# Attention into a mixture of experts: PSUM as four shared tiles of two banks, one eviction over both banks, and a new order

## The chip, the cores and the metric

One core of one Trainium2 chip runs the whole program. The metric is the device time of one execution in microseconds (us). The engines are TensorE (PE: matmuls, with its weight loads as PEld), VectorE (DVE), ScalarE (ACT), GpSimd (POOL) and SyncE (SP), which issues the transfers. Matmul results land in PSUM, which has 8 banks of 512 fp32 values on each of 128 partitions; DVE and ACT copy them on to SBUF. "Quadrants" below are the four 64x64 parts of TensorE's 128x128 array: the half of the partitions that a matmul reads, by the half of the PSUM partitions that it writes.

## The reference

```python
# attention: batch 8, 8 heads, 576 rows, 64 columns a head, fp32
q_d, k_d, v_d = (mean over 4 neighbouring rows of q, k, v)      # 144 pooled rows
out_up    = repeat(softmax(scale * q_d k_d^T) v_d, 4 rows)
out_local = softmax(scale * q k^T where |i - j| < 4) v
x = out_up + out_local                                          # (8, 576, 512)
# mixture of 4 experts of 64 columns, the 2 best of each row by x @ w_gate
q, k, v = x @ wq[e], x @ wk[e], x @ wv[e]
ye = causal_softmax(scale * q k^T) @ v @ wo[e]
out = sum over the two chosen e of w_e * ye
```

## The kernel before

**Stages.** Each of the 8 batches goes through three stages, which run staggered, so that three batches are in work at a time. Stage 1 works on one pair of heads at a time (4 pairs). `s1_local` (L688) makes the banded scores, 20 matmuls of 64 columns. `s1_down` (L725) pools q and k and makes the pooled scores: three query tiles t = 0, 1, 2, each for two heads h, of 144 columns (L773). `s1_out` (L807) transposes both probability tiles ("tp", five blocks of 128x128 each) and multiplies them by v ("o1", "o1d"), which gives x and its split into a high and a low part. Stage 2 projects x to q, k ("pj", L879) and v with the gate ("pv", `s2_v`, L910). Stage 3 is the causal attention: `s2_scores` (L1013), unit u = 1 to 4 of two or three query tiles, `s2_trans` (L1065; "tq", five jobs for each batch and pair of experts), `s2_av` (L1118) and the output projection `s2_out` ("po", L1153; in the last batch `s2_out_cut`, L1171).

**Order.** Every step is an `op` with the engine or engines that may run it, a planned cost, what it reads and writes, and the PSUM and SBUF buffers that it takes. `Plan.schedule` (L245) plays the ops through by these planned costs and writes the instructions in that order, once, when the program is built: of the ops that are ready and whose buffers are free, an engine takes the one of the lowest number in `ORDER`. On TensorE it may prefer another one. An op of the same `MODE` as the last goes ahead if its number is no more than `SWM` above the best (L347), and a change of mode is charged by `SWX` (L376). `MODE` knows "dense" (the projections, on the whole array) and "quarter" (everything on quadrants); the transposes "tp" and "trans", which read one half of the partitions and write all 128, count as "quarter". Where the plan sees too little matmul work, it puts in a filler, a matmul of zeros ("wu", L662).

**PSUM.** There are two pools: `big`, two tiles of two banks (local scores, x, projections, the longest score tile), and `small`, four tiles of one bank (L499 to L503). Pooled scores, transposes and `s2_av` take two small tiles each, one for each half; `s2_v` takes one.

**Evictions.** `transpose` (L553) writes the two halves of a block to two tiles. So each transposed job has two copies to SBUF, `tp_ev` (L816, L826) and `t_ev` (L1115), which the plan gives to ACT or DVE one by one; the copies stand in the profile under the helper's lines, L509 on ACT and L511 on DVE. The pooled scores' maxima are two reductions (L777), one for each small tile.

**The quadrants of the pooled scores.** At L773 head h reads half h of the partitions and writes half h, for each of the three tiles. The local scores swap the heads in half of their tiles (L700), the causal scores in every other tile (L1024).

Of the kernel before, what the change touches and what calls it, by code (L numbers as in the profile page):

```python
# [7 lines left out]
F32 = mybir.dt.float32  # L8
# [451 lines left out]
def dve(n):  # L460
    return 65 + n / 0.96
# [11 lines left out]
def tile_attn_then_moe(ctx: ExitStack, tc: tile.TileContext, qT, kT, v, wqk, wvg, wo, out):  # L473
# [25 lines left out]
    def big(name):  # L499
        return buf(psB, [128, 1024], name, 2, tag="big", fifo=False)  # L500
# [800 lines left out]
```

## Time and profile before

| | |
|---|---|
| time, median of 3 runs | 503.04 us (499.98 to 506.42) |
| the profiled execution's own time | 501.08 us |
| its span, first to last instruction | 499.3 us |
| mean granted TensorE clock | 0.997 of full speed |
| busy share of the span | PE 98%, PEld 85%, DVE 79%, ACT 67%, POOL 63% |

A busy TensorE isn't a TensorE at its peak: a matmul counts as busy for its whole latency, and the next one can start long before it ends. What the engine delivers is read from the distances between starts.

### The profile page before, as it was taken

How to read it: one execution, taken by the hardware profiler on the slowest of the kernel's cores; microseconds unless marked ns; L12 is line 12 of the kernel's file. 1: busy time of each engine (PE TensorE's matmuls, PEld its weight loads, DVE VectorE, ACT ScalarE, POOL GpSimd, SP SyncE). 2: the span in 40 equal slices, each digit the busy share in tenths (PEclk: the TensorE clock that was granted, in tenths of full speed). 3: DMA queues.
4: the chain of work that ended last, by engine and by line, in shares of the span. 5: the costliest groups of instructions: out<-in, count | busy, mean ns of one | idle time of the engine just before them, and what ended most of it. 6: DMA issues, size and time to landing. Idle time of an engine off the chain costs nothing.

```text
span 499.3 us, 20630 instructions
## 1 busy us (share of the span) xinstructions
PE 487.9 (98%) x8391; PEld 423.7 (85%) x8393; DVE 392.2 (79%) x1256; ACT 334.8 (67%) x1150; POOL 314.7 (63%) x451
## 2 busy tenths in 40 slices
PE   8889999999999999999999999999999999999988
PEld 4678997998988988998898888997988888988776
DVE  8899689976867998679887689859995978547770
ACT  2987588767757678556766587656894567455763
POOL 6789968965855689566785468644773664124231
PEclk9989999999999999999999999999999999999999
DMA  8875445431523333242444053414331100100112
GB/s 218 266 210 176 116 131 163 118 99 44 174 90 123 107 114 113 78 152 61 129 123 136 29 152 102 151 55 150 94 123 61 55 1 3 74 26 13 49 51 95
DMA packets 43463, 52.72 MB, mean 106 GB/s; under 512 B 3304, under 2 KB 26344, under 8 KB 43368
## 3 DMA queue, kind: packets, MB, share of 16 engines
q1 hardware_dynamic: 43368, 51.40, 34.6%
q8 instruction: 66, 1.08, 0.9%
q14 instruction: 29, 0.24, 0.1%
HBM read 40.90 MB, written 9.44 MB: 101 GB/s over the span
## 4 chain that ended last, share of the span: by engine, by line
PE 83%; DVE 10%; ACT 3%; DMA 2%; issue 1%; POOL 1%; SPq 0%; DVEq 0%; ACTq 0%; POOLq 0%
PE pj L879 21%; PE po L1160 9%; PE pv L920 9%; PE sq L1024 8%; PE o L1137 6%; PE tq L556 6%; PE tp L556 5%; PE o L838 4%; PE scd L773 4%; PE sc L700 3%; PE o L844 2%; PE pv L929 1%; DVE pr L1042 1%; PE po L1184 1%; DMA wst<-in_wo_dram 1%
## 5 line engine op out<-in xcount | busy, mean ns | idle before, releaser
L1045 ACT ACTIVATE pr<-pr,pst 128x192 f32<-128x192 f32 (+8 forms) x144 | 80.0, 558 | 26.6 <-DVE pst L1042 24.6
L1053 POOL TENSOR_SCALAR pr<-pr,pst,gt 128x192 f32<-128x192 f32 (+8 forms) x88 | 58.7, 671 | 56.7 <-DVE pst L1050 39.6
L879 PE MATMUL pj<-xh,wqk_h 128*128 128x320 f32 (+1 forms) x248 | 77.8, 314 | 0.0
L1042 DVE CUSTOM_DVE_ANT_0 pr<-sq,causal_t 128x192 f32<-128x192 f32 (+8 forms) x144 | 65.8, 483 | 11.2 <-PE sq L1024 10.6
L879 PE MATMUL pj<-xl,wqk_h 128*128 128x320 f32 (+1 forms) x248 | 73.2, 295 | 0.0
L879 PE MATMUL pj<-xh,wqk_l 128*128 128x320 f32 (+1 forms) x248 | 73.1, 295 | 0.0
L1024 PE MATMUL sq<-k,q 64*64 64x256 f32 (+6 forms) x768 | 57.3, 374 | 0.2 <-DVE x L856 0.2
L879 PEld LDWEIGHTS pj<-xh,wqk_h 128*128 128x128 f32 x248 | 46.6, 188 | 4.2 <-issue 1.0
L862 POOL TENSOR_TENSOR xl<-x,xh 128x576 fp32r<-128x576 f32 x29 | 41.3, 1426 | 9.2 <-ACT xh L861 9.2
L879 PEld LDWEIGHTS pj<-xh,wqk_l 128*128 128x128 f32 x248 | 46.7, 188 | 0.0
L879 PEld LDWEIGHTS pj<-xl,wqk_h 128*128 128x128 f32 x248 | 46.6, 188 | 0.0
L785 ACT ACTIVATE dp<-scd,dst 128x144 f32<-128x144 f32 x96 | 35.2, 374 | 10.8 <-DVE dst L780 10.3
L721 POOL TENSOR_TENSOR lp<-lp,lst 128x640 f32<-128x640 f32 x27 | 34.6, 1283 | 10.9 <-DVE lst L720 8.4
L1024 PEld LDWEIGHTS sq<-k,q 64*64 64x64 f32 x768 | 32.2, 133 | 10.8 <-issue 1.0
L556 PE MATMUL tq<-ident,pr 64*128 64x64 f32 x736 | 38.5, 232 | 2.1 <-ACT oh L1148 0.7
L511 DVE COPY ptb<-tq 128x192 f32<-128x192 f32 (+4 forms) x95 | 29.7, 348 | 12.6 <-PE tq L556 12.2
L556 PEld LDWEIGHTS tq<-ident,pr 64*128 64x128 f32 x736 | 29.1, 138 | 11.6 <-issue 3.5
L920 PE MATMUL pv<-wvg_h,xh 128*128 128x260 f32 x128 | 37.5, 293 | 0.0
L1149 POOL TENSOR_TENSOR ol<-oc,oh 128x256 fp32r<-128x256 f32 (+1 forms) x30 | 23.9, 799 | 20.9 <-ACT oh L1148 18.3
L752 POOL TENSOR_TENSOR lr<-lr 128x512 f32<-128x512 f32 x28 | 36.3, 1296 | 0.0
L920 PE MATMUL pv<-wvg_h,xl 128*128 128x260 f32 x128 | 36.2, 283 | 0.0
L920 PE MATMUL pv<-wvg_l,xh 128*128 128x260 f32 x128 | 36.2, 283 | 0.0
(178 smaller groups left out, 1514.5 us busy)
## 6 DMA issues: line engine op xcount, KB each, us to landing
lv<-in_v_dram SPq DMA_DIRECT2D x64, 160.0 KB
lq<-in_qT_dram SPq DMA_DIRECT2D x32, 292.0 KB
lk<-in_kT_dram SPq DMA_DIRECT2D x32, 292.0 KB
out_dram<-ot SPq DMA_DIRECT2D x28, 288.0 KB
lr<-in_v_dram SPq DMA_DIRECT2D x28, 256.0 KB
lr<-in_v_dram SPq DMA_DIRECT2D x28, 64.0 KB
wst<-in_wqk_dram SPq DMA_DIRECT2D x1, 1024.0 KB
vx<-vg SPq DMA_DIRECT2D x8, 128.0 KB
```

Of the source, the lines that this page charges most:

```text
L556: T.transpose(pss[x]()[:, z:z + 64], data[r, 0:128], ident[r, r])
L721: op("l_nrm", "GV", (pool_tt(n), dve(n)), lambda e: eng[e].tensor_tensor(p(), p(), st[:, :, 2:3].to_broadcast([128, NT, W]), op=OP.mult), ...
L752: eng[e].tensor_tensor(vr[:, :, 0:2, :], vr[:, :, 0:2, :], vr[:, :, 2:4, :], op=OP.add)
L785: A.activation(p()[:, t, :], scs[t // 2]()[:, SD * (t % 2):SD * (t % 2) + SD], AF.Exp, bias=st[:, t, 4:5], scale=1.0 / 128.0, accum_out=st ...
L862: op("xl", "GV", (1360, dve(576)), lambda e: eng[e].tensor_tensor(xl(), x(), xh()[:, 0:S].bitcast(F32), op=OP.subtract), r=[x, (xh, 0)], w ...
L879: T.matmul(ps()[:, H0 + n0:H0 + n1], ww[:, c, w0 + 128 * p:w0 + 128 * p + 128], xx[b, c]()[:, n0:n1], start=(i == 0), stop=(i == 3 * NP - 1))
L920: T.matmul(ps()[:, :260], xx[b, c]()[:, 128 * t:128 * t + 128], ww[:, c, :], start=(i == 0), stop=(i == 3 * NP - 1))
L1024: T.matmul(pss[x]()[halves[e ^ (x % 2)], at + to:at + to + n1 - n0], q()[r, 64 * t:64 * t + 64], k()[r, n0:n1], start=True, stop=True)
L1042: op("s_max", "V", dve(n) + 4, lambda x=x, t=t, n=n, src=src: V.tensor_tensor_reduce(rows_of[t], src(), causal_t[:, S - 64:S + 256] if t = ...
L1045: op("s_exp", "A", 281 + n / 1.2, lambda x=x, t=t, n=n: A.activation(rows_of[t], rows_of[t], AF.Exp, bias=st[:, x, 4:5], scale=-1.0, accum ...
L1053: op("s_nrm", "GV", (327 + n / 1.2 + max(0, n - 384) * 1.1, 189 + n / 1.92), lambda g, x=x, t=t, n=n: eng[g].tensor_scalar(rows_of[t], row ...
L1160: T.matmul(ps()[:, H1 + n0:H1 + n1], ww[:, p, 128 * c:128 * c + 128], xx[b, p]()[:, n0:n1], start=(i == 0), stop=(i == 5))
```

## The change

- PSUM is one pool of four tiles of two banks. What took two small tiles takes one tile and uses both banks; `s2_v` puts two of its five row blocks into one tile, one in each bank; scores of units 1 to 3 put their tiles in the two banks of one tile, unit 4 takes two tiles.
- `tp_ev` and `t_ev` are one copy over both banks instead of two. `v_ev` is one copy for two row blocks, and the transfer `v_cp`, which read block 0 and 2 after the third, is issued after the fourth. The pooled maxima are one reduction instead of two.
- In the last pooled query tile the heads are swapped: head h writes half 1 - h. The rows of that tile stand swapped from then on, and the blocks of "pd" are put in another order (`PD0` to `PD4`, `of_head`), so that the products are the same.
- The plan: transposes are a third mode, "column", with its own charges for a change of mode and an `SWM` of 15.6; some planned costs and the fillers' constants differ; `ORDER` is new throughout (2725 numbers before, 2533 after). `SHIFT`, `LU` and the other tables are the same.

```diff
-FR, TGT, TGT0, T0, TGT2, DW = -7.7, 3150.0, 3400.0, 450400.0, 3700.0, 16.5
+FR, TGT, TGT0, T0, TGT2, DW = -1.1, 3150.0, 3400.0, 152400.0, 3700.0, 10.9
...
-MODE = {"local": "quarter", "down": "quarter", "o1": "quarter", "o1d": "quarter", "av": "quarter", "scores": "quarter", "tp": "quarter", "trans": "quarter",
+MODE = {"local": "quarter", "down": "quarter", "o1": "quarter", "o1d": "quarter", "av": "quarter", "scores": "quarter", "tp": "column", "trans": "column",
...
+       (None, "column"): 95.0, ("dense", "column"): 90.0, ("column", None): 100.0, ("column", "dense"): 92.0,
+       ("column", "quarter"): 95.0, ("quarter", None): 165.0, ("quarter", "dense"): 180.0, ("quarter", "column"): 105.0}
+LAG = {"scores": 85.0, "down": 60.0, "local": 50.0, "o1d": 20.0, "tp": 85.0, "trans": 85.0}
-SWM = {None: 5.1, "quarter": 1.6, "column": 4.1, "dense": 4.9}
+SWM = {None: 0.8, "quarter": 1.2, "column": 15.6, "dense": 5.1}
...
-    psB = ctx.enter_context(tc.tile_pool(name="psB", bufs=2, space=bass.MemoryType.PSUM))
-    psT = ctx.enter_context(tc.tile_pool(name="psT", bufs=4, space=bass.MemoryType.PSUM))
+    psB = ctx.enter_context(tc.tile_pool(name="psB", bufs=4, space=bass.MemoryType.PSUM))
...
-    def transpose(pss, z, data):
+    def transpose(ps, z, data):
         for x, r in enumerate(halves):
-            T.transpose(pss[x]()[:, z:z + 64], data[r, 0:128], ident[r, r])
+            T.transpose(ps()[:, 512 * x + z[x]:512 * x + z[x] + 64], data[r, 0:128], ident[r, r])
...
-        op("c_ge", "V", 560, above, r=cks, w=ges, alloc=ges)
-        op("c_pool", "V", 930, fill_pool, r=cks + ges, w=[(PL, 1)])
+        op("c_ge", "V", 1150, above, r=cks, w=ges, alloc=ges)
+        op("c_pool", "V", 2020, fill_pool, r=cks + ges, w=[(PL, 1)])
...
-        scs = [small("scd") for _ in range(2)]
+        scs, at = big("scd"), 512 - SD
...
-                    T.matmul(scs[t // 2]()[r, SD * (t % 2):SD * (t % 2) + SD],
+                    T.matmul(scs()[halves[h ^ (t // 2)], at * t:at * t + SD],
                              qd()[r, min(NQD * t, SD - 64):min(NQD * t, SD - 64) + 64], kd()[r, 0:SD] if t else kd()[r, WT:WT + SD], start=True, stop=True)
-        op("down", "T", 370, mm, r=[qd, kd], w=scs, alloc=scs + [p])
-        for x, n in ((0, 2), (1, 1)):
-            op("d_max", "V", dve(n * SD), lambda x=x, n=n: V.tensor_reduce(
...
+        op("down", "T", 440, mm, r=[qd, kd], w=[scs], alloc=[scs, p])
+        op("d_max", "V", dve(3 * SD), lambda: V.tensor_reduce(
+            scs()[:, 1000:1003], strided(scs()[:, 0:SD], (at, 3)), op=OP.max, axis=AX.X, negate=True), r=[scs], w=[(scs, "m")])
...
-        op("tp", "T", 20 * QT, tr, r=[p], w=pss, alloc=pss + [pt])
-        for x in range(2):
-            op("tp_ev", "AV", (act(5 * TQ), dve(5 * TQ)), lambda e, x=x, pss=pss: copy(
-                e, pt()[:, x], pss[x]()[:, 0:320].rearrange("p (j q) -> p j q", q=64)[:, :, 0:TQ]), r=[pss[x]], w=[(pt, x)])
+        op("tp", "T", 10 * QT + 50, tr, r=[p], w=[ps], alloc=[ps, pt])
+        op("tp_ev", "AV", (act(10 * TQ), dve(10 * TQ)), lambda e, ps=ps: copy(
+            e, pt(), strided(ps()[:, 0:TQ], (512, 2), (64, 5))), r=[ps], w=[pt])
...
-        pss = [(big if t == NU - 1 else small)("sq") for t in ts[:2]]
-        pss += [pss[0]] * (len(ts) - 2)
+        own = [big("sq") for _ in range(2 if u == 4 else 1)]
+        pss = [(own[0], 0), (own[1], 0) if u == 4 else (own[0], 1), (own[0], 0)][:len(ts)]
...
-            for h in range(2):
-                op("t_ev", "AV", (act(k) + m, dve(k) + m), lambda e, h=h, ev=ev: ev(e, h), r=[pss[h]],
-                   w=[(PT[b, p, x[0]], (x[0], x[2], x[3], h ^ x[6])) for x in runs])
+            op("t_ev", "AV", (act(k) + m, dve(k) + m), lambda e, ev=ev: ev(e), r=[ps],
+               w=[(PT[b, p, x[0]], (x[0], x[2], x[3], x[6])) for x in runs])
```

(before the last lines stands `k, m = 128 * len(js), ...` in place of `k, m = 64 * len(js), ...`)

## Rows read from the trace of the kernel before

**Rows 1.** The page's first two parts: busy time of each engine; then, in 40 slices of the span, TensorE's busy share in tenths and its granted clock in tenths of full speed.

```profile
PE 487.9 (98%) x8391; PEld 423.7 (85%) x8393; DVE 392.2 (79%) x1256; ACT 334.8 (67%) x1150; POOL 314.7 (63%) x451
...
PE   8889999999999999999999999999999999999988
...
PEclk9989999999999999999999999999999999999999
```

**Rows 2.** The page's fourth part, the chain that ended last: shares of the span by engine and by line.

```profile
PE 83%; DVE 10%; ACT 3%; DMA 2%; issue 1%; POOL 1%; SPq 0%; DVEq 0%; ACTq 0%; POOLq 0%
PE pj L879 21%; PE po L1160 9%; PE pv L920 9%; PE sq L1024 8%; PE o L1137 6%; PE tq L556 6%; PE tp L556 5%; PE o L838 4%; PE scd L773 4%; PE sc L700 3%; PE o L844 2%; PE pv L929 1%; DVE pr L1042 1%; PE po L1184 1%; DMA wst<-in_wo_dram 1%
```

**Rows 3.** Groups by line, TensorE alone: line, operation, out<-in, shape and count | busy us, mean ns of one | idle time before them and what ended it.

```profile
L556 PE MATMUL tq<-ident,pr 64*128 64x64 f32 x736 | 38.5, 232 | 2.1 <-ACT oh L1148 0.7 <-DVE oc L1146 0.5 <-DVE ptb L511 0.4
...
L773 PE MATMUL scd<-kd,qd 64*64 64x144 f32 x384 | 31.1, 290 | 0.0
...
L556 PE MATMUL tp<-ident,dp 64*128 64x64 f32 x320 | 17.5, 232 | 1.2 <-DVE vd L511 0.8 <-ACT dp L794 0.2 <-DVE pt L511 0.2
L556 PE MATMUL tp<-ident,lp 64*128 64x64 f32 x320 | 16.8, 231 | 0.3 <-DVE pst L1042 0.3
...
L662 PE MATMUL wu<-zero 128*128 128x512 bf16 x36 | 10.0, 398 | 0.1
```

**Rows 4.** The timeline of TensorE, three stretches: start us, length of the merged piece us, line, out<-in, shape, count of instructions. A matmul of fp32 stands as two instructions, its two passes.

```profile
12.99 0.91 PE L773 MATMUL scd<-kd,qd 64*64 64x144 f32 x12
13.83 1.83 PE L758 MATMUL pv<-lv,pool 128*128 128x128 f32 x14
...
202.21 0.26 PE L838 MATMUL o<-pt,lv 64*64 64x58 f32 x1
202.21 0.28 PE L773 MATMUL scd<-kd,qd 64*64 64x144 f32 x1
...
202.33 0.29 PE L773 MATMUL scd<-kd,qd 64*64 64x144 f32 x2
...
203.38 0.47 PE L844 MATMUL o<-pd,vd 64*64 64x144 f32 x8
```

**Rows 5.** The timeline of TensorE again: one job of transposes between quadrant work, two jobs between projections, and the first transposes of the span.

```profile
15.88 0.27 PE L556 MATMUL tp<-ident,dp 64*128 64x64 f32 x1 [0.22 <-ACT dp L794]
...
53.82 0.41 PE L838 MATMUL o<-pt,lv 64*64 64x58 f32 x16
54.16 0.52 PE L556 MATMUL tp<-ident,dp 64*128 64x64 f32 x10
54.61 0.48 PE L844 MATMUL o<-pd,vd 64*64 64x144 f32 x8
...
205.23 0.28 PE L879 MATMUL pj<-xh,wqk_l 128*128 128x256 f32 x1
205.34 0.28 PE L879 MATMUL pj<-xl,wqk_h 128*128 128x256 f32 x1
205.56 0.53 PE L556 MATMUL tp<-ident,dp 64*128 64x64 f32 x10
205.92 0.48 PE L556 MATMUL tp<-ident,lp 64*128 64x64 f32 x10
206.32 0.42 PE L879 MATMUL pj<-xh,wqk_h 128*128 128x320 f32 x1
206.58 0.31 PE L879 MATMUL pj<-xh,wqk_l 128*128 128x320 f32 x1
206.73 0.31 PE L879 MATMUL pj<-xl,wqk_h 128*128 128x320 f32 x1
```

**Rows 6.** Groups by line and form, DVE and ACT: copies out of PSUM and the two reductions of the pooled scores (busy us, mean ns of one | idle before).

```profile
L511 DVE COPY pt<-tp 128x290 f32<-128x290 f32 x35 | 15.1, 451 | 4.9 <-PE tp L556 4.8
L777 DVE TENSOR_REDUCE scd<-scd 128x2 f32<-128x288 f32 x32 | 14.8, 461 | 7.9 <-PE scd L773 5.6 <-ACT dp L785 1.1 <-ACT lp L711 1.0
...
L509 ACT COPY pt<-tp 128x290 f32<-128x290 f32 x29 | 11.1, 404 | 6.1 <-PE tp L556 6.0
...
L509 ACT COPY ot<-po 128x576 f32<-128x576 f32 x17 | 10.8, 638 | 6.3 <-PE po L1160 5.6 <-ACT pr L1045 0.7
...
L777 DVE TENSOR_REDUCE scd<-scd 128x1 f32<-128x144 f32 x32 | 9.8, 306 | 0.2
...
L511 DVE COPY ot<-po 128x576 f32<-128x576 f32 x11 | 8.3, 754 | 1.8 <-PE po L1160 1.2 <-ACT pr L1045 0.3
```

**Rows 7.** The timeline of all engines near the end of the span, where the last batch's transposes stand alone.

```profile
483.19 0.87 PE L556 MATMUL tq<-ident,pr 64*128 64x64 f32 x18 [0.44 <-DVE ptb L511]
483.81 0.82 DVE L511 COPY ptb<-tq 128x320 f32<-128x320 f32 x2 [0.31 <-PE tq L556]
483.85 0.70 ACT L509 COPY ptb<-tq 128x320 f32<-128x320 f32 x2 [0.43 <-PE tq L556]
484.32 0.43 PE L556 MATMUL tq<-ident,pr 64*128 64x64 f32 x6 [0.27 <-ACT ptb L509]
```

**Rows 8.** Busy time of each engine by stretch (PE, PEld, DVE, ACT, POOL, with counts; then the granted clock, the DMA share and GB/s).

```profile
0.00:15.00 15.00, 12.65 (x185) 8.04 (x186) 13.28 (x43) 4.58 (x14) 10.37 (x39) 1.00 0.90 240
...
25.00:30.00 5.00, 3.75 (x72) 3.24 (x70) 3.94 (x10) 4.23 (x15) 3.68 (x4) 0.66 0.84 222
...
480.00:490.00 10.00, 8.15 (x172) 6.51 (x164) 4.79 (x16) 5.54 (x19) 3.65 (x5) 1.00 0.07 24
```

More of the change, by code (lines that the diff above doesn't have):

```diff
@@ L353, in schedule @@
                         best = dense
-                    if e == "T" and free["tr"] + free["big"] > 0 and fill(t, best):
-                        best = self.filler(free["tr"] > 0)
+                    if e == "T" and free["big"] > 0 and fill(t, best):
+                        best = self.filler()
                         left[best.allocs[0]] = 1
@@ L497, in buf, with strided, bank @@
         return b
+    def strided(a, *dims):
+        return bass.AP(tensor=a.tensor, offset=a.offset, ap=[list(a.ap[0])] + [list(d) for d in dims] + [list(a.ap[1])])
     def big(name):
[L500 to L503 removed]
+        return buf(psB, [128, 1024], name, 4, tag="big", fifo=False)
+    def bank(ps, x):
+        return lambda: ps()[:, 512 * x:512 * x + 512]
     eng = {"V": V, "G": G}
@@ L535, in tile_attn_then_moe @@
     V.memset(zero, 0.0)
-    wu = psT.tile([128, 512], F32, name="wu", tag="tr", bufs=4)
+    wu = psB.tile([128, 1024], F32, name="wu", tag="big", bufs=4)
     for _ in range(NW0):
-        T.matmul(wu, zero[:, :128], zero, start=True, stop=True)
+        T.matmul(wu[:, 0:512], zero[:, :128], zero, start=True, stop=True)
     ci = wk.tile([128, 128], I32, name="ci", tag="up")
@@ L656, in needs, with filler @@
         return [(WTS, (id(whi), c)) for c in range(whi.shape[1])]
-    def filler(one):
-        o, ps = Op(), small("wu") if one else big("wub")
+    def filler():
+        o, ps = Op(), big("wu")
         o.kind, o.eng, o.cost, o.prio, o.seq = "warm", "T", 216, 0.0, 0
@@ L801, in s1_down, with of_head, tr @@
         LD[b, c] = (p, vd)
-    def strided(a, *dims):
-        return bass.AP(tensor=a.tensor, offset=a.offset, ap=[list(a.ap[0])] + [list(d) for d in dims] + [list(a.ap[1])])
+    PD0, PD1, PD2, PD3, PD4 = (0, 4), (4, 1), (3, 3), (1, 0), (2, 2)
+    def of_head(a, h, z0, z1, n):
+        a0 = a[:, 5 * h + z0[h], :]
+        return bass.AP(tensor=a0.tensor, offset=a0.offset,
+                       ap=[list(a0.ap[0]), [(z1[h] - z0[h]) * NQD, n], list(a0.ap[1])])
     def s1_out(b, c):
         p, (dp, vd), lv = LP[b, c], LD[b, c], LV[b, c]
-        pss, pt = [small("tp") for _ in halves], buf(wk, [128, 2, 5, TQ], "pt", PTB)
-        def tr(pss=pss):
+        ps, pt = big("tp"), buf(wk, [128, 2, 5, TQ], "pt", PTB)
+        def tr(ps=ps):
@@ L812, in tr @@
             for j in range(5):
-                transpose(pss, 64 * j, p()[:, 2 * j:2 * j + 2, :].rearrange("p t w -> p (t w)"))
-        op("tp", "T", 20 * QT, tr, r=[p], w=pss, alloc=pss + [pt])
-        for x in range(2):
-            op("tp_ev", "AV", (act(5 * TQ), dve(5 * TQ)), lambda e, x=x, pss=pss: copy(
-                e, pt()[:, x], pss[x]()[:, 0:320].rearrange("p (j q) -> p j q", q=64)[:, :, 0:TQ]), r=[pss[x]], w=[(pt, x)])
-        pss, pd = [small("tp") for _ in halves], buf(wk, [128, 2, 5, NQD], "pd", NPD)
@@ L820, in trd @@
-        def trd(pss=pss):
-            flat = dp().rearrange("p t w -> p (t w)")
-            for i, at in enumerate((0, SD + WT, 2 * SD + WT, SD - 64, 2 * SD - 48)):
-                transpose(pss, 80 * i - 16 * (i in (2, 4)), flat[:, at:at + 128])
-        op("tp", "T", 20 * QT, trd, r=[dp], w=pss, alloc=pss + [pd])
-        for x in range(2):
-            op("tp_ev", "AV", (act(5 * NQD), dve(5 * NQD)), lambda e, x=x, pss=pss: copy(
-                e, pd()[:, x], pss[x]()[:, 0:400].rearrange("p (j q) -> p j q", q=80)[:, :, 0:NQD]), r=[pss[x]], w=[(pd, x)])
+                transpose(ps, [64 * j] * 2, p()[:, 2 * j:2 * j + 2, :].rearrange("p t w -> p (t w)"))
@@ L913, in s2_v @@
             op("v_al", "G", 1, lambda: None, alloc=[VG[b]])
-        vg, ps = VG[b], small("pv")
+        if t % 2 == 0:
+            PV[b] = big("pv")
+        vg, ps = VG[b], PV[b]
+        at, first = 512 * (t % 2), [] if t % 2 else [ps]
         def mm(cs):
@@ L937, in s2_v @@
                    r=[(xh[c], 0) for c in cs] + [XL[b, c] for c in cs] + [needs(wvg_h)[c] for c in cs] + [(vg, 9)], w=[ps],
-                   alloc=[ps] if cs[0] == 0 else [])
+                   alloc=first if cs[0] == 0 else [])
         else:
-            op("v", "T", dense(8, 260), mm_tail, r=xh + needs(wvg_h) + [(vg, 9)], w=[ps], alloc=[ps])
-        if t < 4:
-            op("v_ev", "AV", (act(260), dve(260)), lambda e: copy(e, vg()[:, t, :], ps()[:, :260]), r=[ps], w=[(vg, t)])
-        if t == 2:
+            op("v", "T", dense(8, 260), mm_tail, r=xh + needs(wvg_h) + [(vg, 9)], w=[ps], alloc=first)
+        if t in (1, 3):
+            op("v_ev", "AV", (act(520), dve(520)), lambda e: copy(
+                e, vg()[:, t - 1:t + 1, :], ps().rearrange("p (x z) -> p x z", x=2)[:, :, 0:260]), r=[ps], w=[(vg, t - 1), (vg, t)])
+        if t == 3:
             vx = VX[b] = buf(wk, [128, 2, 256], "vx")
@@ L1077, in s2_trans @@
         for js in jobs:
-            pss, first = [small("tq") for _ in halves], []
+            ps, first = big("tq"), []
             parts = sorted(set(place(*x)[0] for x in js))
@@ L1083, in s2_trans, with tr @@
                     first.append(PT[b, p, part])
-            def tr(js=js, pss=pss):
+            def tr(js=js, ps=ps):
                 for x, (t, j) in enumerate(js):
-                    transpose(pss, 64 * x, block(t, j))
+                    transpose(ps, [64 * x] * 2, block(t, j))
             need = sorted(set(y for t, j in js for y in ((t, t - 2) if j == "d" and t < 8 else (t,))))
-            o = op("trans", "T", 4 * QT * len(js), tr, r=[PR[t] for t in need], w=pss, alloc=pss + first)
+            o = op("trans", "T", 2 * QT * len(js) + 50, tr, r=[PR[t] for t in need], w=[ps], alloc=[ps] + first)
             for part in parts:
@@ L1104, in s2_trans, with ev @@
                     runs.append([part, 1, jj, q0, 0, x, t % 2])
-            def ev(eng, h, runs=runs, pss=pss):
+            def ev(eng, runs=runs, ps=ps):
                 for part, n, jj, q0, way, x, odd in runs:
-                    pt, src = PT[b, p, part], pss[h]()[:, 64 * x:64 * (x + n)].rearrange("p (j q) -> p j q", q=64)
-                    if way == 2:
-                        copy(eng, pt()[:, h ^ odd, jj, q0:q0 + 128 * n].rearrange("p (t q) -> p t q", q=128)[:, :, 0:64], src)
-                    else:
-                        copy(eng, pt()[:, h ^ odd, jj:jj + n, q0:q0 + 64], src)
-            k, m = 64 * len(js), 60 * (len(runs) - 1)
-            for h in range(2):
-                op("t_ev", "AV", (act(k) + m, dve(k) + m), lambda e, h=h, ev=ev: ev(e, h), r=[pss[h]],
-                   w=[(PT[b, p, x[0]], (x[0], x[2], x[3], h ^ x[6])) for x in runs])
+                    a = PT[b, p, part]()
+                    step = [a.ap[2][0], 128][way == 2]
+                    src = strided(ps()[:, 64 * x:64 * x + 64], (512, 2), (64, n))
+                    copy(eng, strided(a[:, odd, jj, q0:q0 + 64], (a.ap[1][0] * (1 - 2 * odd), 2), (step, n)), src)
+            k, m = 128 * len(js), 60 * (len(runs) - 1)
+            op("t_ev", "AV", (act(k) + m, dve(k) + m), lambda e, ev=ev: ev(e), r=[ps],
+               w=[(PT[b, p, x[0]], (x[0], x[2], x[3], x[6])) for x in runs])
     def s2_av(b, p, qlo, qhi):
-        vg, vx, obs = VG[b], VX[b], [small("o2") for _ in halves]
+        vg, vx, both = VG[b], VX[b], big("o2")
+        obs = [bank(both, x) for x in range(2)]
         part, n = int(qlo >= CUT), qhi - qlo
-        o, al = buf(wk, [128, 320], "oc"), list(obs)
+        o, al = buf(wk, [128, 320], "oc"), [both]
         al.append(o)
@@ L1173, in s2_out_cut @@
         n = n1 - n0
-        ps = (big if n > 256 else small)("po")
+        ps = big("po")
         one = c not in OT
```

59 lines of the change are left out of this document (31 added, 28 removed), and 266 rows, old and new, of the table ORDER.

## The prediction

> **What bounds the kernel now.** Read the page's busy shares first, and beside them the slices and the granted clock [rows 1]. TensorE is busy for 98% of the span, in every slice after the first three at nine tenths or more until the last two, and the clock stands at its upper level nearly throughout. The next engine, DVE, is busy for 79%. The chain that ended last says the same: 83% of it is TensorE's, spread over all the stages, and 10% is DVE's [rows 2]. So the time is the length of TensorE's stream, and only three things can shorten it: fewer or better overlapped passes, fewer losses between its pieces, fewer waits. Waits that show as idle are few: TensorE lacks 499.3 - 487.9 = 11.4 us of the span. But a matmul counts as busy for its latency, so losses shorter than that are hidden in "busy". They are read from the starts in the timeline of TensorE, which is the view that carries the sum below.
>
> **Heads of the last pooled query tile swapped.** Before, all three tiles use the same two quadrants, one for each head. The call at 12.99 us has 12 passes, in six pairs; its piece is 0.91 us long, one pass 0.29 us [rows 3, 4]. So the six pairs start (0.91 - 0.29) / 5 = 0.124 us apart, and the two other quadrants stand idle. That four quadrants can run side by side at this width is seen in the product of the pooled part: eight passes of 144 columns in 0.47 us, which at the latency of 0.29 leaves 0.18 us between first and last start, for the same two passes in each quadrant [rows 4]. After the swap the third tile's two pairs have quadrants of their own. Four steps are left of six: 2 x 0.124 = 0.25 us a call, and with 32 calls (8 batches, 4 pairs) 8 us. The bounds: 8 us where nothing else used the idle quadrants, 0 if the third tile still starts last or a neighbour already filled them. A neighbour does so now and then: at 202.21 us a matmul of "o1" starts ahead of the last three of the pooled scores [rows 4]. That neighbour's other half must still wait for the two loaded quadrants, so most of the gain remains. I take -7.
>
> The same rows bear on a rule of the Trainium skill that speaks against this size. "TensorE: Matmul & The Clock Gate", part 3 on packing small matmuls, says that matmuls start strictly in program order. By it the third tile's first pair could only run beside the second tile's last, one step saved and not two, this term would be -4 and the forecast 492. The piece at 202.21 us disagrees, since "o1" is later in the program; so the sum stays with the rows.
>
> **Transposes as a mode of their own.** What does one visit to the transposes cost? Inside a run, the next job starts 0.17 us before the one ahead of it ends (205.56 + 0.53 against 205.92), and so does the next projection matmul (205.23 + 0.28 against 205.34) [rows 5]. From quadrant work into a transpose it is only 53.82 + 0.41 - 54.16 = 0.07 us, and out of it 54.16 + 0.52 - 54.61 = 0.07 us: 0.10 us lost each time. The first job after a change takes 0.53 instead of 0.48 us. That is 0.25 us a visit. Between projections: 0.11 lost going in (205.34 + 0.28 - 205.56 = 0.06), 0.05 on the first job, 0.09 coming out (205.92 + 0.48 - 206.32 = 0.08 against 0.17), and the first projection matmul takes 0.42 instead of 0.31: 0.36 us. Counted by order of start through the whole timeline, from 15.88 to 484.32 us, the transposes stand in 118 unbroken visits [rows 5, 7], for 144 jobs (64 "tp", 80 "tq", by the code). At 0.25 to 0.36 us that is 30 to 42 us. The old plan counts a transpose as quadrant work and so mixes them at no charge; the new one charges every change, and stays with transposes while their numbers are up to 15.6 above the best. How many visits go can't be read from the trace, as it depends on how many jobs are ready together. The bounds: at two jobs a visit 46 visits fewer, -13 us at 0.28 us; at one job a visit 26 more, +7 us. 0.28 is near the lower price, as a visit between two different other modes saves only part. I take half of the first, 23 visits, -6.5.
>
> **Evictions over both banks.** A copy of 290 elements takes 451 ns on DVE and 404 on ACT, one of 576 takes 754 and 638 [rows 6]: 1.06 and 0.82 ns an element. One copy of 580 is then some 758 or 641 ns, where two used to run side by side on the two engines: 0.31 or 0.24 us later, 0.27 in the mean. Over 144 jobs that is 39 us if nothing covers it, and 0 if other matmuls always do. The engines gain: one start less for each pair, and one reduction of 432 elements, some 600 ns, for 461 + 306 [rows 6], 5 us in all on DVE. But they have slack, so that is worth nothing on the path. The cover is the other two batches' work: TensorE's idle time before all transposes sums to 2.1 + 1.2 + 0.3 = 3.6 us [rows 3]. Where the cover is gone is the last batch's end: from 480 to 490 us TensorE is busy for 8.15 of 10 us [rows 8], with the last five jobs in it. 5 x 0.27 = 1.4 us; against that, the job at 483.19 waits 0.44 us for a DVE copy and that at 484.32 waits 0.27 us for an ACT copy [rows 7], which I read as waits for a small tile, and four shared tiles would remove them: +0.6. With five more of the other 139 jobs exposed it is +2, which I take.
>
> **Four shared tiles, paired v blocks, the later transfer.** The number of banks is the same, and either use can now take what the other leaves. A pair of v blocks holds its tile for one block longer, and the copy across halves starts one block later; both are hidden by the stages that run between v and `s2_av`. I cost this at 0; a gain from it is rival two, a loss rival four.
>
> **Start and fillers.** In the first 15 us TensorE is idle for 2.35 us, and from 25 to 30 us for 1.25 us, with the granted clock at 0.66: part of that stretch ran at 1.2 instead of 2.4 GHz, 1.7 us lost [rows 8]. 36 fillers take 10.0 us [rows 3]. The new plan has DVE's two steps of constants at twice their former cost, so its first order may fit better. Bounds: -4 (the idle time) to +2 (one more half-speed stretch). I take -1.5.
>
> **The sum.** Against the profiled execution's own 501.08 us: -7 - 6.5 - 1.5 + 2 = -13, so 488.1. The median of the runs is 503.04, 0.4% above the profiled one and inside their spread of 6.4 us; I carry half of that over: 489.
>
> **The rivals.**
> Two: the runs of all three modes get longer, since four interchangeable tiles leave more ready work to choose from. For it: the losses of 30 to 42 us stand next to losses of the same kind between projections and quadrants, which the new charges also weigh. Against it: the charge for those hardly changes. It would take the full -8, -13 and -4, and half of the 1.96: 501.1 - 25 + 1 = 477.
> Three: the change doesn't do what it says on TensorE. Jobs of transposes become ready one at a time, because each waits for its own chain over DVE, ACT and POOL, and 118 jobs out of 144 already stood alone or nearly so; neighbours already filled the idle quadrants. Then -4 to 0 for the swap, -1.5 and +2 as above: 501.1 + 0.5 + 1 = 503 at the most, 499 at the least.
> Four, on the other side: the later copies are exposed. A single copy per job keeps the tile and the products behind it waiting 0.27 us longer, and with one pool a held tile now blocks every other use as well. Without the copies the sum is 487. It is back at 503 when 16 / 0.27 = 59 of the 144 jobs are exposed; 2% slower, 513, needs 26 / 0.27 = 96, and all 144 give 487 + 39 = 526. Against it speak the 3.6 us of idle time today. The Trainium skill points this way too: "TensorEngine Tiling (Array Packing)", section "PSUM Bottleneck", advises to empty PSUM with both ScalarE and VectorE, and after this change each job uses only one; what that costs in this kernel no run here shows yet.
>
> **How the numbers follow.** The forecast, 483 to 495: 0.47. Rival two, 474 to 483: 0.17. Rival three, 495 to 503: 0.20. Rival four, above 503: 0.16, of which 0.10 lies above 513. Two per cent, about what a measurement of this kernel can tell from no change, is below 493 or above 513. Below 493 lie rival two and about five sixths of the forecast: 0.17 + 0.39 = 0.56. Slower is 0.10, and the rest, 0.34, is within. The range from 475 to 502 leaves out little of rival two and rival three and all of rival four, some 0.2. The likeliest case's own range is 483 to 495.
>
> **What the changed profile would show.** The swap: pooled scores of 12 passes in a piece of about 0.66 us instead of 0.91. The grouping: fewer than 100 visits in the timeline of TensorE, the pieces of transposes longer. The copies: half as many under the helper's lines, with means near 0.75 and 0.64 us for "pt", and TensorE's idle time before the products not above today's by more than some 2 us. The forecast is wrong if the visits stay near 118, if the pooled scores keep their 0.124 us steps, or if TensorE's idle time, now 11.4 us, grows by more than a few.

## The result, and the profile after

| | runs | median us | lowest to highest | profiled run / span us |
|---|---|---|---|---|
| before | 4 | 502.67 | 499.98 to 506.42 | 501.08 / 499.3 |
| after | 4 | 485.42 | 481.83 to 488.01 | 483.12 / 481.3 |

The ratio is 0.9647 [0.9548, 0.9746]: faster, by 17 us. A second set of runs of the changed kernel (a0, below) gave 0.9587 [0.9527, 0.9647], 20 us. Where some runs of a kernel were over 1.5% slower than its fastest, at a lower granted clock, its median below is that of the others.

The page of the changed kernel, its first two parts; they answer to [rows 1].

```profile
PE 464.6 (97%) x8401; PEld 410.9 (85%) x8401; DVE 367.0 (76%) x1105; ACT 333.3 (69%) x1055; POOL 318.3 (66%) x461
...
PE   8888998999999999999999999999999999999998
...
PEclk9999997999999999999999999999999999999999
```

TensorE is still the engine that sets the time, with 10 more instructions than before (8401 for 8391: ten more fillers) and 23.3 us less busy time. It lacks 481.3 - 464.6 = 16.7 us of the span now, where it lacked 11.4. So the stream got shorter by more than the kernel gained, and 5.3 us went back into visible waits. The chain of the changed kernel, to be read beside [rows 2], says the same: TensorE's share is down from 83 to 78%, DVE's up from 10 to 12.

```profile
PE 78%; DVE 12%; DMA 3%; ACT 2%; POOL 2%; issue 2%; SPq 1%; DVEq 0%; POOLq 0%; ACTq 0%
```

The groups by line of TensorE, which answer to [rows 3] (L766 was L773, L549 was L556, L655 was L662):

```profile
L549 PE MATMUL tq<-ident,pr 64*128 64x64 f32 x736 | 34.6, 229 | 2.1 <-DVE x L850 0.7 <-DVE ptb L504 0.6 <-DVE pr L1054 0.4
...
L766 PE MATMUL scd<-kd,qd 64*64 64x144 f32 x384 | 22.2, 300 | 0.0
...
L549 PE MATMUL tp<-ident,dp 64*128 64x64 f32 x320 | 16.5, 232 | 0.3
...
L655 PE MATMUL wu<-zero 128*128 128x512 bf16 x50 | 15.2, 414 | 2.1 <-DVE x L850 1.9
...
L549 PE MATMUL tp<-ident,lp 64*128 64x64 f32 x320 | 15.1, 227 | 0.0
```

The pooled scores fell from 31.1 to 22.2 us of busy time although a single pass takes 300 ns and not 290: more of them run at once. The transposes fell from 72.8 to 66.2 us. The fillers rose from 40 to 50 (the 36 "wu" of before and four more that stand there as "wub", 1.5 us), 3.7 us more.

Busy times of overlapping passes don't add up to the span, so the full account goes by starts. Each start-to-next-start distance in the timeline of TensorE is put down to the pass that opens it, and the distances are summed by kind, up to the last product; the 14 fillers behind it take 3.2 us in both kernels.

```
us                     before   after
transposes               67.1    56.8   -10.3
pooled scores            26.4    17.8    -8.6
projections             225.5   221.5    -4.0
local scores             22.4    26.0    +3.6
product with pooled v    16.2    19.5    +3.3
all other               136.3   134.3    -2.0   (last scores and products, fillers, pooling)
```

Counted in the same list, the transposes stand in 58 unbroken visits where it was 118, the quadrant work in 64 runs where it was 121, the projections in 90 before and 62 now. Two visits in the timeline of the changed kernel, with two calls of the pooled scores; the lines at 206 us answer to [rows 5], those at 10.78 and 22.15 to [rows 4]:

```profile
10.78 0.71 PE L766 MATMUL scd<-kd,qd 64*64 64x144 f32 x12
...
22.15 0.66 PE L766 MATMUL scd<-kd,qd 64*64 64x144 f32 x12
...
206.32 0.31 PE L873 MATMUL pj<-xl,wqk_h 128*128 128x320 f32 x1
206.56 0.40 PE L549 MATMUL tq<-ident,pr 64*128 64x64 f32 x6
206.80 0.47 PE L549 MATMUL tp<-ident,lp 64*128 64x64 f32 x10
207.11 0.42 PE L549 MATMUL tq<-ident,pr 64*128 64x64 f32 x8
207.45 0.38 PE L873 MATMUL pj<-xh,wqk_h 128*128 128x256 f32 x1
...
212.21 0.84 PE L549 MATMUL tp<-ident,dp 64*128 64x64 f32 x20
212.89 0.47 PE L549 MATMUL tp<-ident,lp 64*128 64x64 f32 x10
213.20 1.25 PE L549 MATMUL tq<-ident,pr 64*128 64x64 f32 x32
```

A piece of 12 pooled passes is 0.71 or 0.66 us long, by its first step (173 or 125 ns); before, the same two kinds of call took 0.95 and, at 12.99 us, 0.91. A visit now holds three jobs (206.56 to 207.45) or more (212.21 on); in the mean it is 144 / 58 = 2.5.

The copies of "pt" by form, which answer to [rows 6]: 747 and 640 ns for both banks, where 758 and 641 were worked out.

```profile
L504 DVE COPY pt<-tp 128x580 f32<-128x580 f32 x16 | 11.9, 747 | 0.7 <-PE tp L549 0.5
...
L502 ACT COPY pt<-tp 128x580 f32<-128x580 f32 x16 | 10.2, 640 | 3.2 <-PE tp L549 2.9
```

The windows that answer to [rows 8], and the one that holds the slow stretch now:

```profile
0.00:15.00 15.00, 12.71 (x180) 7.06 (x180) 12.67 (x39) 5.83 (x20) 11.87 (x42) 1.00 0.82 232
...
25.00:30.00 5.00, 3.96 (x163) 3.48 (x164) 3.64 (x7) 4.17 (x18) 4.35 (x4) 1.00 0.57 159
...
60.00:120.00 60.00, 57.73 (x1091) 50.36 (x1094) 49.09 (x139) 38.66 (x132) 44.71 (x64) 0.94 0.38 112
```

The first 15 us are as full as before (12.71 for 12.65 us), and the stretch with a lowered clock moved from 25 to 30 us (0.66) into 60 to 120 us (0.94 over the 60 us of that row, 0.7 in one slice of the page). Last, the largest of TensorE's waits in the view of waits, with one further down (what waits <- what it waits for: sum us, count, longest us):

```profile
PE o L831 <- ACT dp L776: 2.3, 2, 1.6
PE wu L655 <- DVE x L850: 1.9, 1, 1.9
PE pv L751 <- DMA lv<-in_v_dram: 1.7, 1, 1.7
PE sc L693 <- issue: 1.5, 3, 0.9
...
PE tq L549 <- DVE x L850: 0.7, 1, 0.7
```

They are few and long, and end on results of ACT and DVE and on one transfer. None of the first four is for a merged copy: all waits of TensorE for copies of transposes sum to 0.9 us, before and after. What is new are waits of 3.0 us for the exponential of the pooled scores ("dp", L776) and 2.9 us for x (L850), by instructions that read neither. What is left for them to wait for is a PSUM tile that those two steps read. Before, the one such wait for x is this, and there is none for "dp":

```profile
PE sq L1024 <- DVE x L856: 0.2, 1, 0.2
```

The fillers' wait for "x" lies at 73 us, in the slice with the lowered clock.

### The profile page after: what moved, and what is told of

Read it like the earlier page. It is cut to its first block, busy times and chain, and to the rows that moved or that the text cites. A ratio compares the mean times of both kernels' runs of the same rounds, so it can differ in the third digit from the quotient of the medians.

```text
span 481.3 us, 20427 instructions
## 1 busy us (share of the span) xinstructions
PE 464.6 (97%) x8401; PEld 410.9 (85%) x8401; DVE 367.0 (76%) x1105; ACT 333.3 (69%) x1055; POOL 318.3 (66%) x461
## 4 chain that ended last, share of the span: by engine, by line
PE 78%; DVE 12%; DMA 3%; ACT 2%; POOL 2%; issue 2%; SPq 1%; DVEq 0%; POOLq 0%; ACTq 0%
PE pj L873 19%; PE pv L919 10%; PE po L1160 9%; PE sq L1025 8%; PE o L1137 7%; PE tq L549 5%; PE o L831 3%; PE tp L549 3%; PE scd L766 3%; PE sc L693 2%; DMA lq<-in_qT_dram 2%; PE wu L655 1%; PE pv L928 1%; PE o L837 1%; DVE x L850 1%
## 5 line engine op out<-in xcount | busy, mean ns | idle before, releaser
L1046 ACT ACTIVATE pr<-pr,pst 128x320 f32<-128x320 f32 (+8 forms) x144 | 79.8, 556 | 16.9 <-DVE pst L1043 15.9
L1054 POOL TENSOR_SCALAR pr<-pr,pst,gt 128x448 f32<-128x448 f32 (+8 forms) x82 | 59.0, 727 | 43.7 <-DVE pst L1051 16.7
L1043 DVE CUSTOM_DVE_ANT_0 pr<-sq,causal_t 128x192 f32<-128x192 f32 (+8 forms) x144 | 64.8, 484 | 18.9 <-PE sq L1025 17.4
L1025 PE MATMUL sq<-k,q 64*64 64x256 f32 (+6 forms) x768 | 54.9, 376 | 0.9 <-DVE x L850 0.4
L776 ACT ACTIVATE dp<-scd,dst 128x144 f32<-128x144 f32 x96 | 35.2, 376 | 24.8 <-DVE dst L771 16.6
L1025 PEld LDWEIGHTS sq<-k,q 64*64 64x64 f32 x768 | 34.7, 134 | 10.8 <-PE sq L1025 1.5
L714 POOL TENSOR_TENSOR lp<-lp,lst 128x640 f32<-128x640 f32 x28 | 35.7, 1280 | 12.1 <-DVE lst L713 11.1
L549 PE MATMUL tq<-ident,pr 64*128 64x64 f32 x736 | 34.6, 229 | 2.1 <-DVE x L850 0.7
L831 PE MATMUL o<-pt,lv 64*64 64x58 f32 (+1 forms) x1280 | 33.4, 224 | 2.3 <-ACT dp L776 2.3
L1054 DVE TENSOR_SCALAR pr<-pr,pst,gt 128x64 f32<-128x64 f32 (+8 forms) x62 | 34.5, 578 | 0.4
L1160 PE MATMUL po<-oh,wo_h 128*128 128x256 f32 (+1 forms) x112 | 34.6, 309 | 0.0
L704 ACT ACTIVATE lp<-lp,lst 128x64 f32<-128x64 f32 x120 | 30.9, 339 | 5.2 <-DVE lst L699 5.1
```

Of the source, the lines that this page charges most:

```text
L549: T.transpose(ps()[:, 512 * x + z[x]:512 * x + z[x] + 64], data[r, 0:128], ident[r, r])
L714: op("l_nrm", "GV", (pool_tt(n), dve(n)), lambda e: eng[e].tensor_tensor(p(), p(), st[:, :, 2:3].to_broadcast([128, NT, W]), op=OP.mult), ...
L776: A.activation(p()[:, t, :], scs()[:, at * t:at * t + SD], AF.Exp, bias=st[:, t, 4:5], scale=1.0 / 128.0, accum_out=st[:, t, 0:1])
L831: T.matmul(o()[r, 512 * x + z:512 * x + z + n], lv()[kr, t, r], pt()[kr, at, t, 0:n], start=True, stop=True)
L1025: T.matmul(pss[x][0]()[halves[e ^ (x % 2)], at_of[x] + at + to:at_of[x] + at + to + n1 - n0], q()[r, 64 * t:64 * t + 64], k()[r, n0:n1], s ...
L1043: op("s_max", "V", dve(n) + 4, lambda x=x, t=t, n=n, src=src: V.tensor_tensor_reduce(rows_of[t], src(), causal_t[:, S - 64:S + 256] if t = ...
```

## The experiments

The theory: the gain is TensorE's, the swap (about 8 us) and 60 visits fewer at about 0.25 us (15 us), less 5 us of new waits. The rival: it comes from copies over both banks, which spare DVE 25 us of work, and from four tiles of one kind. Unless said otherwise a time stands beside a0, runs of the changed kernel itself: 482.44 us, 0.9587 [0.9527, 0.9647].

**a0_after_again**: no edit.

> The changed kernel once more, on the chip on which the next three run: 482 to 488 us on every theory. The other three are compared with this one.

**e1_heads_back**: the heads of the third tile go back to the quadrants of the others, everything else and the order stay.

```diff
-                    T.matmul(scs()[halves[h ^ (t // 2)], at * t:at * t + SD],
+                    T.matmul(scs()[halves[h], at * t:at * t + SD],
...
-    PD0, PD1, PD2, PD3, PD4 = (0, 4), (4, 1), (3, 3), (1, 0), (2, 2)
+    PD0, PD1, PD2, PD3, PD4 = (0, 0), (1, 1), (2, 2), (3, 3), (4, 4)
...
-                         of_head(pd()[lo], h, PD3, [PD4[1] + 5, PD4[0] - 5], 2), start=False, stop=True)
+                         of_head(pd()[lo], h, PD3, PD4, 2), start=False, stop=True)
```

> The changed kernel with the heads of the last pooled query tile back in their own quadrants; the order of all instructions stays. Theory (the third tile's two pairs ran beside the first tile's): +8 us over the changed kernel (32 calls, 0.25 us each). By matmuls that start strictly in program order: +4. If neighbours had filled the idle quadrants anyway: 0 to +1.

Measured: 488.02 us, 0.9686 [0.9639, 0.9732], so the swap is worth 5.6 us by the medians (0.0099 x 502 = 5.0 by the ratios). By the time alone the two expectations can't be told apart, as 5 to 5.6 lies between +8 and +4; the starts decide. Its timeline and its group by line:

```profile
7.86 0.95 PE L766 MATMUL scd<-kd,qd 64*64 64x144 f32 x12
...
L766 PE MATMUL scd<-kd,qd 64*64 64x144 f32 x384 | 29.5, 286 | 0.1
```

The piece is 0.95 us long, against 0.71. The single starts in an undisturbed call, in ns after its first, show why:

```
e1:    0 7  173 180  296 302  418 425  540 547  663 670
after: 0 7   27  33  173 180  200 207  296 302  418 425
```

With the swap, the passes of the third tile (at 27 and 200) start beside those of the first, not behind those of the second; the call's last start comes 245 ns earlier, as worked out. Which pass is which is told by the call's signal to the other engines, which the last pass in the program carries: that pass is the 12th to start in 28 of the 32 calls of e1, and the 8th in 27 of 32 of the changed kernel. By the sums over starts the pooled scores take 24.8 us in e1 and 18.9 in a0, 5.9 less, and the product with pooled v 18.4 and 19.4, 1.0 more.

**e6_before_swap**: the swap alone, put into the kernel before with its old order, by the same edits the other way round.

> The kernel before with nothing but the heads of the last pooled query tile swapped; the order of all instructions is that of before. Theory: -6 us against the kernel before, as undoing it cost 5.6. By a strict start in program order: -4. If the rest of the change is needed for it: 0.

Measured: 497.67 us, 0.9898 [0.9825, 0.9972], 4 to 5 us. The pooled scores fall from 26.4 to 19.1 us, and the product with pooled v rises from 16.2 to 17.3. Both ways round, then, the pooled scores give 5.9 to 7.3 us, and the product gives back 1.0 to 1.1 of it.

**e2_quarter_between** adds work: ahead of each job of transposes one tiny matmul in a single quadrant (4 columns, into an unused corner). In the inner 144 - 58 = 86 places this is a change of mode and back; in 37 others, ahead of the first job after a projection, it puts quadrant work in between.

```diff
+    def tiny(ps):
+        T.matmul(ps()[lo, 504:508], zero[lo, 0:64], zero[lo, 0:4], start=True, stop=True)
...
         def tr(ps=ps):
+            tiny(ps)
```

(one of three such places)

> The changed kernel with one matmul of 4 columns, on one quadrant, put ahead of each of the 144 jobs of transposes; nothing else moves in the order. So the 58 visits to the transposes become 144. Theory (a visit costs 0.25 to 0.36 us, and the fewer visits are what made the kernel faster): 86 more visits at 0.25 to 0.30, and some 38 changes from projections that now pass through a quadrant at 0.1 to 0.2: +25 to +34 us over the changed kernel. Rival (visits cost little, the gain came from copies that relieve DVE and ACT): +4 to +8 us, the passes alone.

**e3_column_between**: the same tiny matmul in the shape of the transposes, 64 rows by 128 columns.

```diff
+        T.matmul(ps()[:, 504:508], zero[lo, 0:128], zero[lo, 0:4], start=True, stop=True)
```

> The control: the same small matmul ahead of each job, but as wide as a transpose (64 partitions read, 128 written), so that the number of visits stays at 58. Both theories: 0 to +8 us over the changed kernel, which is the price of 144 passes alone.

Measured: e2 502.8 us, 0.9985 [0.9948, 1.0022]; e3 481.08 us, 0.9574 [0.9521, 0.9626]. The instruction costs nothing (-1.4 us, inside the spread); the change of shape costs 20.3 us, less than the 25 to 34 expected. Where it costs is read from the distance between the last start ahead of the tiny matmul and the job's first start behind it, over all jobs: in the 86 inner places 272 ns in e2 and 36 in e3 (medians), 0.24 us each, 19.3 us in sum; in the 37 places behind a projection 332 and 221 ns, 0.11 us each, 4.4 us in sum. (The profiled run took 509.18 us, so these two sums can't be held against the 20.3 to a microsecond.) In the timeline of e2, the three jobs that stand at 206.56 us in the changed kernel:

```profile
216.28 0.19 PE L552 MATMUL tq<-zero 64*64 64x4 bf16 x1
216.40 0.40 PE L549 MATMUL tq<-ident,pr 64*128 64x64 f32 x6
216.73 0.19 PE L552 MATMUL tp<-zero 64*64 64x4 bf16 x1
216.85 0.53 PE L549 MATMUL tp<-ident,lp 64*128 64x64 f32 x10
217.31 0.19 PE L552 MATMUL tq<-zero 64*64 64x4 bf16 x1
217.43 0.46 PE L549 MATMUL tq<-ident,pr 64*128 64x64 f32 x8
217.82 0.39 PE L878 MATMUL pj<-xh,wqk_h 128*128 128x256 f32 x1
```

From job to job it is 0.45 and 0.58 us, where it was 0.24 and 0.31: 0.21 and 0.27 us for going out and back. The clock stood at its upper level in this stretch. So the price of a visit, read from single lines before, is nearly right, and the 60 visits fewer are worth 60 times 0.22 (19.3 / 86) to 0.24 us, 13 to 14 us.

**e8_after_quarter**: transposes are planned as quadrant work again, the rest as changed. The planner was run anew, with the tuned numbers of the changed kernel's order. The end of a long line:

```diff
-"tp": "column", "trans": "column",
+"tp": "quarter", "trans": "quarter",
```

> The changed kernel, but the plan counts transposes as quadrant work again; tiles, copies and ORDER as changed. The plan, played through anew, has 89 visits to the transposes and 262 changes of mode. Theory (0.12 us a change): +8 us over the changed kernel. Rival (the plan's view of the mode doesn't matter, only tiles and copies): within 2 us.

Measured: 499.06 us, 0.9957 [0.9933, 0.9981], 14 to 17 us more than the two medians of the changed kernel. It has 89 visits, 31 more; at 0.24 us they make 7. Some 3 us of the rest show as waits: distances between starts of over 400 ns, each less 250, sum to 18.2 us in the changed kernel (11.4 before) and 21.4 here. What is left is not accounted for. So it points the way of the theory, but as a size it is spoilt: the order's numbers were fitted to another plan.

**e4_split_copies** and **e5_two_pools** were run in the same manner, the plan made anew: in e4 each job has two copies again, one for each bank, free to go to either engine; in e5 the four tiles are two pools of two.

```diff
+        for x in range(2):
+            op(("tp_ev", "tp_ev2")[x], "AV", (act(5 * TQ), dve(5 * TQ)), lambda e, x=x, ps=ps: copy(
+                e, pt()[:, x], strided(ps()[:, 512 * x:512 * x + TQ], (64, 5))), r=[ps], w=[(pt, x)])
...
-        return buf(psB, [128, 1024], name, 4, tag="big", fifo=False)
+        return buf(psB, [128, 1024], name, 2, tag="big" if name in ("sc", "o1", "pj", "po", "sq8") else "sm", fifo=False)
```

> The changed kernel with the copies of the transposes split again, one for each bank, each free to go to ACT or DVE; one tile of two banks as before, and ORDER unchanged (the second copy has the number of the first). The plan, played through anew, has 61 visits to the transposes instead of 58 and 223 changes of mode instead of 198. Theory (the time follows the changes of mode, 0.12 us each, and a merged copy is worth little by itself): +3 us over the changed kernel's 482 to 485. Rival one (the copies that were saved are what made it faster): +8 us or more. Rival two (the merged copy comes late and causes the new waits): -3 us or faster.

> The changed kernel with its four tiles in two groups of two: local scores, x, the projections and the longest score tile in one, all else in the other, as it was before. ORDER unchanged, the plan played through anew: 95 visits to the transposes instead of 58, 333 changes of mode instead of 198, 96 fillers and warming matmuls instead of 57. Theory (freely shared tiles are what lets the runs of one mode get long; 0.12 us a change): 135 more changes, +16 us, and up to +5 for fillers where they don't lie in waits: 498 to 505. Rival (the mode of its own in the plan is enough): within 4 us of the changed kernel.

Measured: e4 509.1 us, 1.0145 [1.0108, 1.0182]; e5 554.03 us, 1.103 [1.0947, 1.1114]. The theory missed both by 20 us and more; taken by its own words, e4 speaks for its rival one (+8 or more). But the long distances sum to 33.0 and 53.9 us, and e5 has 89 fillers for 50. These are poor plans, and what of their time is the edit's can't be told: they price neither the merged copies nor the shared tiles. What they do give is a count: in this order there are 89 visits without the mode of its own (e8) and 95 without the shared tiles (e5), against 58 with both. The three runs taught to keep the order fixed, which the rest do.

**e9_both_engines** and **e10_same_engine**: the order stays, each merged copy becomes two halves. In e10 both run on the engine of the merged one, in e9 the second half runs on the other engine. One of the places:

```diff
-            e, pt(), strided(ps()[:, 0:TQ], (512, 2), (64, 5))), r=[ps], w=[pt])
+            second(e, x), pt()[:, x], strided(ps()[:, 512 * x:512 * x + TQ], (64, 5))) for x in range(2)], r=[ps], w=[pt])
```

> The changed kernel with every instruction in its place, but the copy of each transposed job split in two by bank: one half stays on its engine, the other goes to the other of ACT and DVE at the same place in the order. If the later landing of the one long copy causes the new waits: -2 to -6 us against the changed kernel (ratio to the kernel before 0.950 to 0.957). Rival (the other engine is busy with something else at that moment and now stands ahead of its own work; relief of DVE and ACT is worth something): +2 to +10 us.

> As the run before, but both halves stay on the engine that had the long copy, one behind the other: the merging alone is undone, in number of instructions. If the start of an instruction counts: two copies of 290 elements for one of 580 cost some 0.06 to 0.15 us of the engine, 144 times, 9 to 22 us over both engines, of which a small part is on the path: +1 to +4 us. If it is covered: 0.

Measured: e10 487.05 us, 0.967 [0.9635, 0.9704], 1 to 4 us more by the two ratios of the changed kernel; e9 538.0 us, 1.0696 [1.0668, 1.0724], 51 us more than e10, which neither of its expectations had. The copies of e9 are shorter, and yet it is the slowest run with this order. Its chain, the wait of TensorE that is largest in sum, and the largest waits of DVE and of ACT:

```profile
PE 55%; DVE 21%; ACT 16%; issue 3%; DMA 2%; POOL 2%; SPq 1%; POOLq 0%; ACTq 0%; DVEq 0%
...
PE o L1141 <- DVE ptb L504: 6.2, 6, 1.7
...
DVE ptb L504 <- ACT ptb L502: 35.4, 59, 4.2
...
ACT ptb L502 <- DVE ptb L504: 28.3, 52, 1.9
```

DVE and ACT hold 37% of the chain instead of 14%, and they wait for each other. In all 64 "tp" jobs the second half starts only when the first, on the other engine, has ended, 31 ns after it at the least. DVE waits 78.7 us in sum for halves on ACT, and ACT 59.3 us for halves on DVE; in e10 and in the changed kernel no copy of a transposed job waits for the other engine's. So e9 did not put the halves side by side. Why the second waits is not shown; both read one tile, whereas in the kernel before, with a tile for each half, they overlapped [rows 7]. From the start of a job's last pass to the end of its copies it is some 0.9 us more than in the changed kernel. And e9's mean granted clock is 0.971, against 1.00 in the profiled run of e10: some 15 us of the 51, an estimate from (1 - 0.971) x 536.

**e12_late_copies** adds work: ahead of each merged copy the same engine copies the job's first block alone (it is written again by the merged one). So each product gets its operand later, and the order stays.

```diff
-            e, pt(), strided(ps()[:, 0:TQ], (512, 2), (64, 5))), r=[ps], w=[pt])
+            e, pt()[:, :, 0, :], strided(ps()[:, 0:TQ], (512, 2))), copy(
+            e, pt(), strided(ps()[:, 0:TQ], (512, 2), (64, 5)))], r=[ps], w=[pt])
```

> The changed kernel with every instruction in its place, but ahead of each long copy of a transposed job the same engine makes a copy of its first block alone (64 columns of each bank at most, 0.12 to 0.2 us more of the engine, by the copies' 1.06 and 0.82 ns an element and the runs' copies of 128). So all 144 copies land later by about that. If the lateness of the copies is not covered by other work (the prediction's fourth rival): 144 times 0.12 to 0.2, +17 to +29 us over the changed kernel. If it is covered as forecast (about ten jobs exposed): +1 to +4 us, with the engines' extra load.

Measured: 495.6 us, 0.985 [0.9792, 0.9907], 10 to 13 us more by the two ratios of the changed kernel. The copies by form, and the chain:

```profile
L504 DVE COPY pt<-tp 128x580 f32<-128x580 f32 x16 | 12.2, 762 | 0.5
...
L504 DVE COPY pt<-tp 128x116 f32<-128x116 f32 x16 | 4.2, 263 | 1.4 <-PE tp L549 1.3
```

```profile
PE 72%; DVE 15%; ACT 6%; DMA 3%; issue 3%; POOL 1%; SPq 0%; ACTq 0%; DVEq 0%; POOLq 0%
```

The added copy takes 263 ns and not the 120 to 200 of the expectation. From the start of a job's last pass to the end of its copies it is 1.39 us ("pt") and 1.26 ("pd") in the median, 0.34 us more than in the changed kernel. Over 144 jobs that is 48 us, of which a fifth to a quarter reach the end: a late copy here is covered in part only, and costs 0.07 to 0.09 us a job. The engines' extra load is in this price too.

**e11_no_tail**: the fillers that stand behind the last product are left out.

```diff
-    for o in plan.schedule():
+    placed = plan.schedule()
+    end = max(i for i, o in enumerate(placed) if o.who == "T" and o.kind != "warm")
+    for o in [o for i, o in enumerate(placed) if o.kind != "warm" or i < end]:
```

> The changed kernel without the 14 fillers behind its last product. They end later than the last copy; if they set the end of the span: -1 to -1.5 us. If the last transfer and its confirmation set it: 0.

Measured: 481.08 us, 0.9574 [0.9539, 0.961]. That is 1.4 us below a0 by the medians and not to be told from it by the intervals. No run here is clearly faster than the changed kernel.

## Why the prediction held, and where it did not

Faster was right, and 485.4 lies between the forecast of 489 and the 477 of rival two. That the sum came so near is in part luck: errors of opposite sign met.

**The swap, -7 forecast, -4 to -5.6 measured (e6, e1).** The mechanism was right: four steps for six, the last start 245 ns earlier. The length forecast for the piece, 0.66 us, holds for calls like the one that it was read from (22.15 us); other calls start with a step of 173 ns and not 125, and take 0.71, where they took 0.95 before. The pooled scores alone give 5.9 to 7.3 us, but the product with pooled v takes 1.0 to 1.1 us longer in both pairs of runs. What makes it longer was not tried. The rule that the prediction weighed, that of the Trainium skill in "TensorE: Matmul & The Clock Gate", part 3, would have the third tile start behind the second; the starts at 27 and 200 ns, ahead of the second tile's at 296, speak against it for passes on other quadrants.

**Transposes as a mode of their own, -6.5 forecast, -13 to -14 by count and price.** The price of 0.25 to 0.36 us a visit was near: 0.22 to 0.24 by e2, with e3 as the control that it is the shape and not the instruction. The step that failed is the count. "At two jobs a visit 46 visits fewer" was set as the far bound, and half of it was taken; it came to 60 fewer, 2.5 jobs a visit. The runs of the other two modes grew along with it (121 to 64 and 90 to 62), as rival two had it. Whether the charges or the shared tiles did that no run separates; by the counts of e8 and e5 it took both in this order. The trace of before could not give the count, but nothing in it bounded a visit at two jobs, and a bound has to be set by what a row excludes.

**Evictions, +2 forecast.** The length of the copies came out to 11 ns. But the step that had them land 0.27 us later failed: it let the two copies of every job run side by side before. In the trace of before only 38 of the 64 "tp" jobs have their copies on two engines. From the start of a job's last pass to the end of its copies it is 1.00 us ("pt") and 0.88 ("pd") in the median before, and 1.06 and 0.92 after: 0.05 us later. Over 144 jobs that is 7 us and not 39, and at e12's share some 2 us, an estimate. So the +2 stands by this sum, though not for the reason given; that nearly all copies are covered, e12 contradicts. Undoing the merging on one engine costs 1 to 4 us (e10); against copies on two engines at once no run shows its worth, as the halves of e9 don't overlap and e4 needs another order.

**Four shared tiles, 0 forecast.** This is the term that was too good. TensorE's idle time grew by 5.3 us, which comes near the prediction's own sign of being wrong ("by more than a few"). By the view of waits it went into the waits for a tile that "dp" or x read: 5.9 us, against 0.2 before. That is the second half of rival four, a held tile that blocks other uses. It is read from what each instruction reads and waits for; no run tested it.

**Start, -1.5 forecast: nothing gained.** TensorE is busy for 12.71 instead of 12.65 us of the first 15, the slow stretch came back later and cost more (60 x 0.06 = 3.6 us for 1.7), and there are ten fillers more.

**Together**: -4 to -5.6 for the swap, -13 to -14 for the visits, +5.3 for the waits make -12 to -14, against the -17 measured, or -20 by a0. So 3 to 8 us are not accounted for. A candidate is the changes between projections and quadrant work with no transposes in between, 63 where it was 92: at the 0.11 us of e2's 37 places 29 fewer make 3 us, an estimate that no run tested.

**The rival cause, relief of DVE, is at most a small part.** DVE's busy time fell by 25 us, but DVE was not what TensorE waited for: TensorE's waits that DVE ended sum to 5.2 us before and 5.6 after. e10 gives the second start back to every copy, 3.9 of those 25 us, and loses 1 to 4 us; the rest no run undid. Rival three is refuted by e1 and by the count of visits; of rival four, late copies do cost (e12), but the merged ones are hardly later. The sentence of the Trainium skill beside it, "TensorEngine Tiling (Array Packing)", section "PSUM Bottleneck", to empty PSUM with both engines, is followed here job by job: of the copies of "pt" 16 are on each engine. Whether the halves of one job side by side would do better no run here shows.

**Open** are how much of the gain four tiles of one kind bring and how much the new order, what merging is worth against copies on two engines at once, and the 3 to 8 us.

## What to carry to other kernels

When matmuls of different tile shapes share TensorE, count the unbroken visits in its timeline and price one by a tiny matmul put between two jobs, with one of the same shape as the control; count times price is the gain to be had, and its upper end is not two jobs a visit. Try parts of a planned kernel with its order held fixed: an order fitted to one plan and replayed on another cost up to 70 us, of which the edit's own part could not be read. Before a step is taken as side by side, look in the trace whether it was: the copies that merging was to make later had shared an engine in 26 of 64 jobs, and the halves of e9, meant to overlap, ran one behind the other.

## What the runs showed of the hardware that was not expected

- Passes on other quadrants start ahead of earlier ones in the program: the third tile's first pass starts 27 ns after the call's first, the second tile's at 296, and the pass that carries the call's signal, its last in the program, is the 8th of 12 to start in 27 of 32 calls.
- A matmul of 4 columns between transposes costs nothing in their own shape (e3) and 0.24 us in a quadrant's (e2); between a projection and a transpose a quadrant's costs 0.11 us.
- The spread from run to run of the changed kernel goes with the granted clock, though not in proportion: 481.83 us at a mean of 0.996, 483.12 at 0.993, 487.72 at 0.989, 488.01 at 0.982.
